# Loading the last three chunks of x by one transfer per partition quadrant, and issuing the first chunk from ScalarE

## The chip, the cores and the metric

One core of a Trainium2 chip. Times are microseconds of device time for one execution; lower is better. The profile's span (first to last instruction) is about 1.7 us shorter than the time.

## The reference, cut to what matters

```python
# x: (1, 384, 384, 384) bf16, dw: (1, 1, 384) bf16, pw: (384, 384) bf16
out = x * dw[0, 0]                          # k = 1: the depthwise part is a scaling of channels
return einsum('bhwc,cd->bhwd', out, pw)     # 147456 rows of 384 channels, times 384 x 384
```

113 MB come in and 113 MB go out. dw is folded into pw once, so the work is one large matrix product, read and written once.

## The kernel before

The 147456 rows are 288 supertiles of 512 rows. They are loaded and stored in chunks: groups of 1, 1, 2, 2, 4 supertiles at the start, tens in the middle, then 6, 4 and 3, 2, 1, 1, 1 at the end. Three x buffers and three output buffers, of ten supertiles each, are used in turn. VectorE transposes, TensorE multiplies, ScalarE evicts (copies the results from PSUM to the output buffer), and SyncE issues nearly all transfers, in program order on one queue. The code is cut and condensed.

```python
head, tail = [[1, 1, 2, 2, 4]], [[6, 4], [3, 2, 1, 1, 1]]
LMAX = 10; NR = 3; LONG = 3
...
def load_x(t):
    g, i, off, first, L = chunks[t]
    dst = Xs[g % NR][:, 4 * off : 4 * (off + L), :]
    rows = xf[512 * first : 512 * (first + L), :]
    if first + LONG < NS:
        src = rows.rearrange("(p s) c -> p (s c)", p=P)
        dst = dst.rearrange("p s c -> p (s c)")
    else:                                    # the last three chunks: rows of 768 B
        src = rows.rearrange("(a k q) c -> q a k c", k=4, q=4)
    if i == 0 and g >= NR:                   # until the buffer's old rows are transposed
        nc.sync.wait_ge(...)
    nc.sync.dma_start(dst, src).then_inc(s_x[g % NR][i], 16)

def store(t):
    ...
    nc.sync.wait_ge(s_a[je % 2], je // 2 + 2)          # the eviction of its last supertile
    nc.sync.dma_start(dst, src).then_inc(s_o[g % NR], 16)

nc.scalar.dma_start(dw_row[:], ...).then_inc(s_dw, 16)
nc.sync.dma_start(pw_n[:], ...).then_inc(s_pw, 16)
# then all loads and stores on nc.sync: a load when the group three before it is done,
# a store two supertiles after its chunk; at the end SyncE waits for all stores
for o in range(NR):
    nc.sync.wait_ge(s_o[o], 16 * sum(map(len, groups[o::NR])))
```

The last three chunks hold their rows in another order, so that their stores are contiguous (3072 B from each partition). Their loads pay for it with rows of 768 B.

## Time and profile before

| | before |
|---|---|
| time, median of the first three runs | 575.39 us |
| span of the profiled run | 573.7 us |
| TensorE's stream of 13824 matmuls | 7.18 to 569.0 us, idle 0.1 us |
| last eviction ends | 569.96 us |
| SyncE's wait for the stores at the very end | 2.0 us |

### The profile page before, as it was taken

The numbers are of one execution on the slowest core, as the hardware profiler recorded it, in microseconds if no ns is written. First come the engines' busy times: TensorE is split into PE (matmuls) and PEld (weight loads), VectorE is DVE, ScalarE is ACT, GpSimd is POOL, SyncE is SP. The second block draws the span as 40 slices with busy tenths as digits, with TensorE's granted clock in tenths as the row PEclk, the third lists the DMA queues.
The fourth block names the chain that finished last, engine by engine and source line by source line (L and its number), as shares of the span: only waits on it lengthen the run. The fifth ranks groups of instructions, "written<-read, shape, count | busy, mean of one in ns | idle before, by whom it ended". The sixth has DMA issues, their size and how long they took to land.

```text
span 573.7 us, 29706 instructions
## 1 busy us (share of the span) xinstructions
PE 567.3 (99%) x13869; PEld 414.9 (72%) x13869; DVE 509.3 (89%) x583; ACT 418.8 (73%) x296; POOL 0.9 (0%) x8
## 2 busy tenths in 40 slices
PE   8999999999999999999999999999999999999996
PEld 5777777777777777777777777777777777777774
DVE  6899999999999999999999999999999999999994
ACT  6777777777777777777777777777777777777775
POOL 0000000000000000000000000000000000000000
PEclk9999999999999999999999999999999999999999
DMA  8999999999999999999999999999999999994996
GB/s 324 432 409 417 430 397 430 444 424 422 399 408 416 384 397 436 398 383 395 432 398 384 395 429 390 393 401 429 402 385 419 401 390 397 425 394 149 402 408 251
DMA packets 25912, 226.88 MB, mean 395 GB/s; under 512 B 1197, under 2 KB 5678, under 8 KB 22062
## 3 DMA queue, kind: packets, MB, share of 16 engines
q1 hardware_dynamic: 25900, 226.79, 98.0%
q14 instruction: 9, 0.07, 0.0%
q8 instruction: 1, 0.02, 0.0%
q10 hardware_dynamic: 2, 0.00, 0.0%
HBM read 113.54 MB, written 113.25 MB: 395 GB/s over the span
## 4 chain that ended last, share of the span: by engine, by line
PE 98%; DMA 1%; ACT 0%; DVE 0%; issue 0%; SPq 0%
PE ps L166 97%; DMA pw_n<-in_pw_dram 1%; PE ps L216 1%; DMA out_dram<-O 0%; ACT O L307 0%; DVE O L304 0%; SPq L337 0%; SPq L100 0%
## 5 line engine op out<-in xcount | busy, mean ns | idle before, releaser
L166 PE MATMUL ps<-w_r,T 32*128 32x384 bf16 x13824 | 561.8, 321 | 0.1
L258 DVE STREAM_TRANSPOSE T<-X 128x384 uint32<-128x384 uint32 x576 | 506.2, 882 | 54.0 <-DMA X<-in_x_dram 2.4
L307 ACT CAST O<-ps 128x1536 bf16<-128x1536 f32 x288 | 413.5, 1436 | 147.9 <-PE ps L166 147.9
L166 PEld LDWEIGHTS ps<-w_r,T 32*128 32x128 bf16 x13824 | 412.9, 93 | 149.2 <-issue 0.7
L271 ACT CAST w_r<-ps 128x768 bf16<-128x768 f32 x5 | 3.7, 805 | 1.7 <-PE ps L216 1.6
L183 PE MATMUL ps<-zero 32*128 32x384 bf16 x24 | 2.6, 494 | 1.4 <-POOL zero L232 1.4
L304 DVE CAST O<-ps 128x768 bf16<-128x768 f32 x1 | 1.0, 958 | 3.0 <-DMA out_dram<-O 3.0
L216 PE MATMUL ps<-pw_n,sel_w 64*128 64x384 bf16 x18 | 3.0, 510 | 0.1
L183 PEld LDWEIGHTS ps<-zero 32*128 32x128 bf16 x24 | 0.7, 100 | 2.6 <-issue 2.6
L216 PEld LDWEIGHTS ps<-pw_n,sel_w 64*128 64x128 bf16 x18 | 1.2, 138 | 1.6 <-issue 1.2
L244 ACT ACT_TABLE_LOAD x1 | 1.3, 1283 | 1.5 <-SPq L100 1.5
L276 DVE TENSOR_REDUCE sel<-eye 128x64 f32<-128x128 bf16 x1 | 0.3, 290 | 1.8 <-POOL eye L234 1.8
L271 DVE CAST w_r<-ps 128x768 bf16<-128x768 f32 x1 | 1.0, 956 | 1.0 <-PE ps L216 1.0
L286 DVE TENSOR_SCALAR sel_w<-sel,dw_f 128x256 bf16<-128x256 f32 x3 | 0.9, 348 | 0.0
L283 DVE COPY dw_f<-ps 128x3 f32<-128x3 f32 x1 | 0.2, 161 | 0.8 <-PE ps L198 0.8
L198 PEld LDWEIGHTS ps<-ones,dw_row 1*128 1x128 bf16 x3 | 0.2, 98 | 0.2 <-issue 0.2
L244 ACT COPY warm<-warm 128x1 f32<-128x1 f32 x2 | 0.3, 188 | 0.0
L234 POOL TENSOR_SCALAR_AFFINE_SELECT eye<-ones 128x128 bf16<-128x128 bf16 x1 | 0.3, 292 | 0.1
L232 POOL MEMSET zero<- 128x192 uint32 x1 | 0.3, 258 | 0.0
L198 PE MATMUL ps<-ones,dw_row 1*128 1x1 bf16 x3 | 0.2, 159 | 0.0
L233 POOL MEMSET ones<- 128x128 bf16 x1 | 0.2, 204 | 0.0
L231 POOL MEMSET warm<- 128x3 f32 x1 | 0.1, 101 | 0.5 <-SPq L100 0.5
(4 smaller groups left out, 0.4 us busy)
## 6 DMA issues: line engine op xcount, KB each, us to landing
X<-in_x_dram SPq DMA_DIRECT2D x26, 3840.0 KB, 21.5
out_dram<-O SPq DMA_DIRECT2D x26, 3840.0 KB, 27.5
X<-in_x_dram SPq DMA_DIRECT2D x2, 1536.0 KB, 17.4
out_dram<-O SPq DMA_DIRECT2D x2, 1536.0 KB, 13.7
X<-in_x_dram SPq DMA_DIRECT2D x3, 768.0 KB, 8.8
out_dram<-O SPq DMA_DIRECT2D x3, 768.0 KB, 8.9
X<-in_x_dram SPq DMA_DIRECT2D x1, 2304.0 KB, 18.9
out_dram<-O SPq DMA_DIRECT2D x1, 2304.0 KB, 12.1
```

The source lines that it names most:

```text
L166: mm = nc.tensor.matmul(PS[s][:, q, :D], lhsT=Ts[s][32 * q : 32 * q + 32, b, par::2], rhs=w_r[32 * q : 32 * q + 32, b, par, :], start=(b, ...
L183: nc.tensor.matmul(PS[0][:, i, :D], lhsT=zero[32 * i : 32 * i + 32, 0:P], rhs=zero[32 * i : 32 * i + 32, :], start=True, stop=True, tile_p ...
L198: mm = nc.tensor.matmul(PS[1][:, 0, D + k : D + k + 1], lhsT=dw_row[:, P * k : P * k + P], rhs=ones[0:1, 0:1], start=True, stop=True,)
L216: mm = nc.tensor.matmul(PS[(k + 1) % 2][:, 2 * r + v, :D], lhsT=sel_w[64 * v : 64 * v + 64, k, r, :, :].rearrange("p q w -> p (q w)"), rhs ...
L232: nc.gpsimd.memset(zero[:].bitcast(U32), 0).then_inc(s_zero)
L234: nc.gpsimd.affine_select(out=eye[:], in_=ones[:], pattern=[[-1, P]], compare_op=mybir.AluOpType.is_equal, fill=0.0, base=0, channel_multi ...
L244: c = nc.scalar.copy(warm[:, s + 1 : s + 2], warm[:, 0:1])
L258: ins = nc.vector.transpose(out=Tw[:, 3 * h : 3 * h + 3], in_=Xw[:, :, j, 96 * h : 96 * h + 96].rearrange("p k (b w) -> p b k w", w=32),)
L271: o = nc.vector.tensor_copy(out, in_) if e == 0 else nc.scalar.copy(out, in_)
L286: nc.vector.tensor_scalar_mul(sel_w[:, k], sel[:].unsqueeze(2).to_broadcast([P, 2, 4, 32]), dw_f[:, k : k + 1]).then_inc(s_sw)
L304: e = nc.vector.tensor_copy(Ov[:, nq:4, j, :], PS[s][:, nq:4, :D])
L307: a = nc.scalar.copy(Ov[:, 0:nq, j, :], PS[s][:, 0:nq, :D])
```

## The change

The intent: the old loads of the last three chunks have q = 4 as slowest source dimension and run on four DMA engines, in a stretch in which the DMA moves 100 GB/s. With one transfer per quadrant (32 partitions) each runs on sixteen. The first chunk of x is issued by ScalarE, so that it need not wait behind pw's issue on SyncE.

```diff
-        def load_x(t):
+        def load_x(t, eng=nc.sync):
...
+            if first + LONG < NS:
+                src = rows.rearrange("(p s) c -> p (s c)", p=P)
+                eng.dma_start(dst.rearrange("p s c -> p (s c)"), src).then_inc(sem, 16)
+            else:
+                src = rows.rearrange("(a k q) c -> q a k c", k=4, q=4)
+                for q in range(4):
+                    nc.sync.dma_start(dst[32 * q : 32 * q + 32], src[q]).then_inc(sem, 16)
...
         nc.scalar.dma_start(dw_row[:], dw.rearrange("a e c -> a (e c)")).then_inc(s_dw, 16)
+        load_x(0, nc.scalar)
         nc.sync.dma_start(pw_n[:], pw.rearrange("(k p) d -> p k d", p=P)).then_inc(s_pw, 16)
...
-                    nc.vector.wait_ge(s_x[g % NR][i], 16 * sum(len(ls) > i for ls in groups[g % NR : g + 1 : NR]))
+                    nc.vector.wait_ge(s_x[g % NR][i], x_count[t])      # 64 per quadrant-loaded chunk
```

More of the change, by code (lines that the diff above doesn't have):

```diff
@@ L60 @@
     NT = len(chunks)
+    x_count = []
+    for t, (g, i, off, first, L) in enumerate(chunks):
+        n = 4 if first + LONG >= NS else 1
+        x_count.append(16 * n + max([x_count[u] for u in range(t) if chunks[u][0] % NR == g % NR and chunks[u][1] == i], default=0))
     g_end = [max(c[3] + c[4] for c in chunks if c[0] == g) - 1 for g in range(len(groups))]
@@ L104, in load_x @@
             rows = xf[512 * first : 512 * (first + L), :]
-            if first + LONG < NS:
-                src = rows.rearrange("(p s) c -> p (s c)", p=P)
-                dst = dst.rearrange("p s c -> p (s c)")
-            else:
-                src = rows.rearrange("(a k q) c -> q a k c", k=4, q=4)
+            sem = s_x[g % NR][i]
             if i == 0 and g >= NR:
@@ L112, in load_x @@
                 nc.sync.wait_ge(s_t[je % 2][1], je // 2 + 1)
-            nc.sync.dma_start(dst, src).then_inc(s_x[g % NR][i], 16)
+            if first + LONG < NS:
[5 more added lines that the diff above has]
+                    nc.sync.dma_start(dst[32 * q : 32 * q + 32], src[q]).then_inc(sem, 16)
         def store(t):
@@ L135 @@
         for t, (g, i, off, first, L) in enumerate(chunks):
-            todo.append((g_end[g - NR] if g >= NR else -1, load_x, t))
+            if t > 0:
+                todo.append((g_end[g - NR] if g >= NR else -1, load_x, t))
             todo.append((first + L + 1, store, t))
```

## The prediction

> **What bounds the kernel now.** I read the page first, then the chain of work that ended last, then the timeline of the first 16 us and the DMA view of the start and of the last 60 us, because the change touches only those two ends. From the page:
>
> ```profile
> span 573.7 us, 29706 instructions
> ...
> PE 567.3 (99%) x13869; PEld 414.9 (72%) x13869; DVE 509.3 (89%) x583; ACT 418.8 (73%) x296; POOL 0.9 (0%) x8
> ...
> L166 PE MATMUL ps<-w_r,T 32*128 32x384 bf16 x13824 | 561.8, 321 | 0.1
> L258 DVE STREAM_TRANSPOSE T<-X 128x384 uint32<-128x384 uint32 x576 | 506.2, 882 | 54.0 <-DMA X<-in_x_dram 2.4
> ```
>
> The matmul stream covers 561.8 of 573.7 us and its column of idle time holds 0.1 us. So nothing in the middle is waiting for x. The transposes idle 54.0 us, but only 2.4 of these for x, all near the start. The chain of waits in order of time gives the rest:
>
> ```profile
> 1.01 3.03 DMA pw_n<-in_pw_dram
> ...
> 4.09 2.96 PE ps L216 x18
> 7.05 0.12 issue
> 7.18 557.91 PE ps L166 x13728
> ...
> 566.57 2.46 DMA out_dram<-O
> 569.02 0.94 DVE O L304
> ```
>
> The end is: load of pw (1.01 to 4.04), 18 matmuls that build w_r (to 7.05), start of the stream at 7.18, 288 supertiles, last eviction, last store. A supertile is 557.91 us for 13728 matmuls of 48, thus 557.91 / 286 = 1.951 us. 7.18 + 288 x 1.951 = 569.0, which is where the last eviction starts (569.02, 0.94 long). The two-digit DMA step before it is an attribution to whichever semaphore came last; the eviction can only start when the matmuls are done, and it does so at just that time. After 569.96 come the last store's issue (570.06), its landing 2.3 us later and a close of about 1.3 us. The timed median is 575.39, 1.7 us over the span. So the time is: start of the stream + 561.8 + about 4.7 + 1.7. The change can act only on the start of the stream, on a stall inside it, or on the last store.
>
> The timeline of the start shows that the first chunk of x is not what starts the stream:
>
> ```profile
> 1.52 3.49 SPq L113 DMA_DIRECT2D X<-in_x_dram  x7
> ...
> 4.63 3.80 ACT L271 CAST w_r<-ps 128x768 bf16<-128x768 f32 x5 [1.56 <-PE ps L216]
> 4.96 0.96 DVE L271 CAST w_r<-ps 128x768 bf16<-128x768 f32 x1 [1.00 <-PE ps L216]
> 5.83 1.55 DVE L258 STREAM_TRANSPOSE T<-X 128x384 uint32<-128x384 uint32 x2
> ...
> 8.00 1.57 DVE L258 STREAM_TRANSPOSE T<-X 128x384 uint32<-128x384 uint32 x2 [0.62 <-DMA X<-in_x_dram]
> ```
>
> The first transposes follow VectorE's own cast of w_r without idle time; x's first chunk landed 3.5 us after its issue at 1.52, so at 5.0. The second chunk made VectorE wait 0.62 us, yet supertile 1 starts only at 9.13 and needs its first half of T by then; 8.00 + 0.88 (one transpose) = 8.9 is in time.
>
> The last three chunks: engine busy time by stretch, whose last two columns are the DMA share and GB/s:
>
> ```profile
> 516.00:520.00 4.00, 4.00 (x104) 2.95 (x100) 3.63 (x5) 2.88 (x2) 0.00 (x0) 1.00 0.78 309
> 520.00:524.00 4.00, 4.00 (x108) 2.94 (x100) 3.63 (x5) 2.88 (x2) 0.00 (x0) 1.00 0.31 89
> 524.00:528.00 4.00, 4.00 (x105) 2.93 (x101) 3.61 (x5) 2.88 (x2) 0.00 (x0) 1.00 0.34 99
> ```
>
> For some 12 us the DMA moves about 100 GB/s, with a share of 0.31 to 0.34, about five engines of 16, while TensorE is full. That is a large defect that costs nothing: the stream is at its full rate through it.
>
> **What the Trainium skill says.** "DMA: Bandwidth & Descriptors", section "Why a DMA increments its semaphore by 16 and not by 1", says that the number of DMA engines used is the largest one up to 16 that divides the slowest dimension of both access patterns. The old source has q = 4 slowest, so 4 engines; the new ones have 32 rows, so 16. The trace agrees: share 0.31, and 3 x 393 KB at about 100 GB/s is 11.8 us, as long as the dip. The same page, "Issuing engines are not separate DMA queues", says that transfers issued by different engines share the 16 DMA engines and that only issue time is saved. The trace of before has one load per queue at a time and can't show it. Its section "Queues, rings and completion order" says that each DMA engine takes turns between the queue rows it has work for; no run here shows it yet, and it is my main concern. "TensorE: Matmul & The Clock Gate", Part 1, says the array runs at half clock until a window of about 3.4 us was busy. The trace agrees in kind: the 18 building matmuls go in pairs 2.96 / 9 = 0.33 us apart, while four stream matmuls take 1.951 / 12 = 0.163 us, at equal width of 384 columns.
>
> **The change part by part.** First, the tail. Three issues become twelve. A load's issue takes about 0.45 us, so nine more are about 4 us on SyncE's queue. But one of the three old issues was held for 8.8 us and one for 4.4, and the five of that group took 14.91 us (511.42 to 526.33). I expect the new ones to be out by about 518, so the store behind them goes out some 8 us sooner than at 526.38. The loads should land about 10 us sooner. They are needed at about 559, two supertiles before their matmuls (7.18 + 285 x 1.951 = 563), and landed by about 532: 27 us of slack already. Stores do not gain at the end either: the last three small stores land 3.3, 2.6 and 2.3 us after issue, so the queue has no backlog by then. Worth to the time: 0, at most 0.1 us.
>
> Second, the start. What is removed is one issue (0.45 us) of SyncE, so that the chunks from the second on go out 0.5 us sooner; VectorE's 0.62 us wait shrinks, and TensorE does not notice: 0. What is added to ScalarE is one issue of 0.49 us (as for dw_row) ahead of its table load (1.49, 1.28 us) and two copies: ScalarE is ready at 3.6 and not at 3.1, and its first cast comes at 4.63: 0. The chunk itself is issued at 0.97 + 0.49 = 1.46 and not at 1.52: no gain.
>
> What moves is the order on the DMA engines. Before, x's first chunk stood behind pw on one queue. Now it stands on another. pw is the head of the critical chain, and of its packets only some have gone when the chunk comes:
>
> ```profile
> DMA packets 132, 0.10 MB, mean 169 GB/s; under 512 B 0, under 2 KB 132, under 8 KB 132
> ## 3 DMA queue, kind: packets, MB, share of 16 engines
> q1 hardware_dynamic: 132, 0.10, 75.3%
> ```
>
> This is 2.2 to 2.8 us. dw_row's packets came about 0.9 us after its issue began, so the chunk's should come at about 2.4 to 2.5. By then pw has moved 14 + some 66 of its 384 packets of 768 B; about 304 are left, 19 per engine. The chunk is 8 packets of 3072 B per engine, each about 0.124 us (81 packets at a share of 104.8% of 16 engines in 4.0 to 4.6 us). If the engines alternate, all eight go ahead of pw's last: 8 x 0.124 = 1.0 us later for pw, and so for the stream. If the engine prefers the older ring or the chunk starts later, less. I take 0.6 as the middle. Sum: tail 0, issue 0, sharing +0.6, so 575.39 + 0.6 = 576.0.
>
> **The rivals.** (a) Nothing: pw's descriptors are all queued before the chunk's, and the engines finish them first. For it: its issue ends at 1.46, when ScalarE's second begins. Then 575.3 to 575.5. (b) Full alternation: 576.4. (c) The clock: TensorE's filler ends at 4.02, just before pw lands at 4.04; a pause of up to 1 us there may cost the busy window, and the stream would start at half clock. The building matmuls ran slow until about 6.6 and the stream fast from its first, so the switch came late. Up to 3.4 us at half speed loses 1.7 us: 577 to 578 at worst. Against it: the pause is under a third of a window. (d) Gain: pw at the head of a less crowded queue, or a better place of the clock window: 575.0. (e) The tail as the bound: excluded by the full matmul stream in 520 to 528. A loss of 2% would be 11.5 us, more than the whole head before the stream; a gain of 2% would need the stream itself to speed up, which has no idle time to give.
>
> **Range and chances.** Weights of about a third each for nothing, part and full alternation, a fifth for some clock loss on top, a tenth for a small gain: 576.0, range 575.1 to 577.3. Within 2%: 0.985; faster 0.005; slower 0.01.
>
> **What would show it right or wrong.** Right: pw lands later than 3.03 us after issue by as much as the stream starts later than 7.18; packets on both queues between 2.4 and 4 us; still 1.951 us a supertile; the 520 to 528 dip gone, with no effect on the end. Wrong: pw at 3.0 us again (rival a); matmuls of the stream slow at first (c); a wait of TensorE on transposes in the stream; a last store that lands sooner or later by over 0.3 us.

## More of the kernel before

The queue's own waits of the kernel before (waiting engine and line, releaser: us in total, times, longest):

```profile
SPq L141 <- DMA out_dram<-O: 2.0, 1, 2.0
```

It is one wait, after the last issue, for all stores to land. It is the last piece of the span that the kernel's own work decides.

## The result, and the profile after

| | before | after |
|---|---|---|
| time, median (6 runs each) | 575.44 us | 577.26 us (577.11 to 577.34) |
| span of the profiled run | 573.7 us | 575.5 us |
| stream of matmuls starts | 7.18 us | 7.22 us |
| last eviction ends | 569.96 us | 570.01 us |
| SyncE's wait for the stores | 2.0 us | 3.7 us |

The ratio is 1.003, with a 95% interval of 1.0017 to 1.0043. A ratio is the mean time of the fast runs of one kernel over that of the other's of the same rounds, so not quite the ratio of the medians quoted. The change is 1.8 us slower: far inside 2%, but clear of the noise.

The chain of waits of the kernel after, in order of time (start, length, what):

```profile
1.03 3.06 DMA pw_n<-in_pw_dram
...
4.13 3.01 PE ps L225 x18
7.14 0.07 issue
7.22 557.91 PE ps L175 x13728
...
569.07 0.94 DVE O L313
```

Up to the last eviction it is the old chain, 0.04 us later: pw landed after 3.06 us, where it took 3.03. So almost all of the 1.8 us come after 570 us. The queue's own waits of the kernel after:

```profile
SPq L150 <- DMA out_dram<-O: 3.7, 1, 3.7
```

3.7 against 2.0 us in this last wait, plus 0.04 at the start, is the difference, but for rounding. The DMA view of 569 to 571 us shows whose landing it is (size, then us from issue to landing). Before:

```profile
out_dram<-O SPq DMA_DIRECT2D x1, 384.0 KB, 2.3
```

After:

```profile
out_dram<-O SPq DMA_DIRECT2D x1, 384.0 KB, 4.1
```

The same 384 KB, issued at 570.06 and 570.10 us, land 1.8 us later. Engine busy time by stretch of the kernel after (last columns: TensorE clock, DMA share, GB/s):

```profile
516.00:520.00 4.00, 4.00 (x107) 2.96 (x100) 3.63 (x5) 2.88 (x2) 0.00 (x0) 1.00 1.03 331
520.00:524.00 4.00, 4.00 (x108) 2.92 (x103) 3.63 (x5) 2.88 (x2) 0.00 (x0) 1.00 0.64 151
524.00:528.00 4.00, 4.00 (x104) 2.95 (x100) 3.63 (x5) 2.88 (x2) 0.00 (x0) 1.00 0.24 75
```

The dip that the change was to fill is still there. And SyncE's timeline shows that the twelve issues were not quick. Before:

```profile
511.42 14.91 SPq L113 DMA_DIRECT2D X<-in_x_dram  x5
526.38 4.41 SPq L128 DMA_DIRECT2D out_dram<-O  x1
```

After:

```profile
511.46 0.81 SPq L116 DMA_DIRECT2D X<-in_x_dram  x2
512.32 16.43 SPq L120 DMA_DIRECT2D X<-in_x_dram  x12
528.79 0.58 SPq L135 DMA_DIRECT2D out_dram<-O  x1
```

The twelve took 16.43 us, and the store behind them went out at 528.79, 2.4 us later than before.

Why should a store be slow at 570 when the loads were over at 535? The landing of a transfer is the last of its increments, and the trace has the time of each increment: sixteen for a transfer on sixteen DMA engines, one when each engine's share has landed. I sorted them. For the five transfers that matter, the first fifteen and the last stand like this (us; worked out from the increments in the two traces):

```text
                                  before                       after
transfer                     issued  15th   16th         issued  15th   16th
store, 3840 KB               476.9   496.1  505.4        476.9   497.0  505.0
load, three supertiles       511.4   519.1  528.7        511.5   520.9  528.4
store, 3840 KB               526.4   543.5  544.5        528.8   539.9  545.2
store, 3840 KB               535.4   552.6  553.6        535.4   549.3  555.7
last store, 384 KB           570.1   572.3  572.4        570.1   572.4  574.2
```

In both kernels one increment comes 6 to 10 us after the other fifteen, from the middle of the run on. In the kernel before this lag is all but gone after the four-engine loads. In the kernel after it is 5 to 6 us there and still 1.8 us at the last store (574.175 less 572.380). So the theory, L: **one DMA engine lags behind the other fifteen. The old loads used four engines, and this one was not among them; so it could catch up while they ran. The new ones give it a sixteenth of everything.** In the trace of the kernel after, each of the twelve quadrant loads has one late increment, the first of them at 530.9 and the last at 534.75 us. The transfer ahead of them was done on that engine at 530.7. So its share of the three chunks cost it 4.07 us.

The packed traces also hold the DMA packets, without the names of their engines, and they show the same. Between 522.5 and 526.4 us of the kernel before, 367 packets of 768 B (the four-engine loads) fill the time of 3.9 engines, and 12 packets of 9216 and 7680 B, of the transfers ahead of them, come one after the other, 0.32 to 0.36 us apart, and fill that of one more. In the kernel after, 12 packets of 3072 B come one at a time, 0.12 us apart, from 572.36 us on; 0.4 us after the end of the last one the last store has landed.

### The profile page after: what moved, and what is told of

Its sections match the earlier page's. It is cut to its first block, busy times and chain, and to the rows that moved or that the text cites. A ratio compares the mean times of both kernels' runs of the same rounds, so it can differ in the third digit from the quotient of the medians.

```text
span 575.5 us, 29715 instructions
## 1 busy us (share of the span) xinstructions
PE 567.4 (99%) x13869; PEld 415.0 (72%) x13869; DVE 510.9 (89%) x583; ACT 418.8 (73%) x296; POOL 0.9 (0%) x8
## 4 chain that ended last, share of the span: by engine, by line
PE 97%; DMA 1%; ACT 0%; DVE 0%; issue 0%; SPq 0%
PE ps L175 97%; DMA pw_n<-in_pw_dram 1%; PE ps L225 1%; DMA out_dram<-O 0%; ACT O L316 0%; DVE O L313 0%; SPq L346 0%; SPq L105 0%
```

## The experiments

The rivals were H (the second queue at the start costs the time), F (the form of a quadrant load costs, whichever engine), I (what costs is that the store behind the loads is issued late) and M (there is no single engine; it changes). Twelve kernels ran, in four calls; each call has its own runs of the kernel before, with medians of 575.53 to 575.61 us. All were correct.

| run | what | median us | ratio to before | last wait of SyncE, profiled run |
|---|---|---|---|---|
| e1 | ScalarE's issue alone | 575.86 | 0.9998 | 2.8 |
| e2 | quadrant loads alone | 577.39 | 1.0022 | 4.0 |
| e3 | quadrants, last chunk | 576.09 | 1.0002 | 2.4 |
| e4 | quadrants, last two | 576.48 | 1.0009 | 3.1 |
| f2 | e2, last stores on 15 engines | 578.32 | 1.0046 | 4.4 |
| f3 | e2, two quadrant loads doubled | 580.27 | 1.0073 | 6.9 |
| f4 | e2, a store ahead of the loads | 577.79 | 1.0031 | 5.1 |
| h1 | e2, pair load on 4 engines | 576.24 | 1.0008 | 3.0 |
| h2 | e2, pair load on 5 engines | 581.24 | 1.0095 | 8.0 |
| h3 | before, pair load on 4 engines | 580.18 | 1.0080 | 5.4 |

f1 and g1 are probes with one look each.

### e1_scalar_issue_only and e2_quadrants_only: which half of the change

e1 keeps the single transfers at the end; e2 takes the other half:

```diff
# e1
-        n = 4 if first + LONG >= NS else 1
+        n = 4 if first + QUAD >= NS else 1          # QUAD = 0: no chunk by quadrants
# e2
-        load_x(0, nc.scalar)
-            if t > 0:
-                todo.append((... load_x, t))
+            todo.append((... load_x, t))
```

> Only the first chunk's issue moves to ScalarE; the last three loads stay single transfers. Theory L (one DMA engine lags the other 15 by about 8 us in the steady state; the old four-engine loads left it out and let it catch up, the sixteen-engine loads don't): 575.4 to 575.5 us, start of the stream at 7.2, last store landing at 572.4. Rival H (the second queue costs the time, for example by sharing at the start or by a lasting disturbance of the rings): 577.2 us.

> Only the last three loads change; the first chunk is issued by SyncE as before. Theory L: 577.2 us (576.9 to 577.4), the last store's sixteenth landing 1.5 to 2 us after its fifteenth-but-one, last eviction still at 569.0. Rival H: 575.4 us.

e1 measured 575.86 us, ratio 0.9998, somewhat above L's 575.4 to 575.5; e2 577.39 us, ratio 1.0022 (1.0000 to 1.0043). H falls: the quadrant loads alone make the time of the whole change. The last wait in e2:

```profile
SPq L148 <- DMA out_dram<-O: 4.0, 1, 4.0
```

e1's four runs go from 575.52 to 576.64. Its profiled run (576.08 us) has a lag of 0.8 us at the last store, so the old form does not clear the lag fully in every run either. The runs of the kernel before scatter in the same way, 575.38 to 577.7.

### e3_quadrants_last_one and e4_quadrants_last_two: the dose

```diff
+                if first + QUAD >= NS:              # QUAD = 1, 2
+                    for q in range(4):
+                        nc.sync.dma_start(dst[32 * q : 32 * q + 32], src[q]).then_inc(sem, 16)
+                else:
+                    nc.sync.dma_start(dst, src).then_inc(sem, 16)
```

> Quadrant loads for the last chunk alone, the two before it as single four-engine transfers. Theory L: each chunk by quadrants costs the lagging engine 4.07/3 = 1.36 us (it needed 530.7 to 534.75 us for its share of three), so two fewer take 2.7 us off a lag of 1.8 at the end: none left, 575.4 to 575.6 us. Rival F (the form of the load, four issues and four waits of the last chunk, costs by itself): most of the 1.8 us, 576.5 to 577.2.

> Quadrant loads for the last two chunks. Theory L: 1.36 us less than for three: 575.7 to 576.1 us. Rival F: the same as with three, 577.2.

The medians are 576.09, 576.48 and (e2) 577.39 us for one, two and three chunks, beside 575.59 for none. The order is that of L, and F's step at the first chunk is absent. But one chunk cost 0.5 us, where L as I wrote it said 575.4 to 575.6 us and so 0.0 to 0.2, and two cost 0.9, where it said 575.7 to 576.1 us and so 0.3 to 0.7. The simple count of 1.36 us per chunk overstates what leaving one out gives back; the old form's own scatter (e1) may be a part of that. The intervals (for e3, 0.998 to 1.0025) are wider than these steps, so the order rests on the medians and on the last waits, 2.4 and 3.1 us.

### f1_width_probes and g1_width_probes_fine: which engine

Eight small loads of n rows to an unused tile, each with its own semaphore, ahead of the last three chunks. The reading of them takes it that a wider probe uses the engines of a narrower one and more:

```diff
+            if first + LONG == NS:
+                for w, n in enumerate(WIDTHS):
+                    some = rows.rearrange("(a k) c -> a k c", k=4)[:n, 0]
+                    nc.sync.dma_start(scratch[:n, w], some).then_inc(s_probe[w], 16)
```

> The kernel before with eight tiny extra loads (2, 4, 8, 10, 12, 14, 15 and 16 rows of 768 B to an unused tile) issued just before the last three chunks; only their landings matter, not the time. Theory L: one ring is still busy until about 530 us with the two loads ahead; [...]all probes that leave the lagging engine out land by about 523 us and all that include it at about 530 us or later. The step tells which engine it is, above the lowest four. Rival M (no single engine; the late increment is on changing engines): no such step, or late landings in the narrow probes too.

> The same probes with 3, 4, 5, 6, 7, 8, 9 and 16 rows. The first probes put the late landing between 4 rows (none) and 8 rows (one at 532.6 us), so the lagging engine is one of the fifth to eighth. Theory L: one step between two neighbouring widths, with exactly one landing after 530 us in every wider probe. If it lies between 7 and 8 rows, it is the eighth engine, number 7.

Increments of each probe, from the two traces; an early increment at the issue, which each probe but the one of 16 rows has, is left out:

```text
rows                           2   3   4   5   6   7   8   9  10  12  14  15  16
landings before 526 us         2   3   4   4   5   6   7   8   9  11  13  14  15
landings after 532 us          0   0   0   1   1   1   1   1   1   1   1   1   1
```

There is exactly one late landing in every probe of five rows and more, and none in those of four and fewer, in both runs (on 4, 8, 10 and 16 rows, which both have, they agree). A single step fits that order. So it is one engine, and in the order in which engines are used it is the fifth. M falls for these two runs, which were on two chips (15 and 7), so it is not a fault of one chip alone. The four-engine loads of the kernel before leave it out by one place.

f1's single time was 577.53 us with the last eviction 0.9 us later than before. It was not run for its time.

### f2_last_stores_fifteen: a wrong guess at the engine

Sent in the same call as f1, before I knew its answer; I had guessed the highest engine.

```diff
+                nc.sync.dma_start(dst[:120], src[:120]).then_inc(s_o[g % NR], 16)
+                nc.sync.dma_start(dst[120:], src[120:]).then_inc(s_o[g % NR], 16)
```

> Quadrant loads for three chunks as in the change, first chunk by SyncE; the last three stores are cut into 120 rows and 8 rows, so that the highest DMA engine has no part in them. Theory L with the highest engine as the lagging one: the lag has 3 x 0.98 us less to do, the end no longer waits for it: 575.7 to 576.0 us (one more issue of 0.35 us at the end). If the lagging engine is another one: 577.5 to 577.8 us.

578.32 us: not the highest engine. It is even 0.5 us above the range for that case. That fits what f1 showed: the fifth engine takes 8 of the 120 rows and one of the 8, so nine packets and not eight in each of the three stores. But no run isolates this.

### f3_quadrants_doubled: twice the suspected cost

```diff
+                for q in range(4 if first + 2 >= NS else 0):
+                    nc.sync.dma_start(dup[NS - 1 - first][32 * q : 32 * q + 32], src[q]).then_inc(s_dup, 16)
```

> Quadrant loads for three chunks, and the last two of them a second time to an unused tile. Theory L: two more chunk shares of 1.36 us on the lagging engine, which is never idle from there to the end: 577.2 + 2.7 = 579.9 us, about 2.2 us of tolerance for its idle time. Rival I (what costs is that the store behind the loads is issued late, 528.8 instead of 526.4): eight more issues of 0.6 us, nothing proportional, and the other fifteen engines late too.

580.27 us against 579.9 expected. The last wait grew to 6.9 us. At the last store of the profiled run fifteen engines had landed by 574.1 us and the lagging one by 577.7, so in the main it is the one engine, though the others were over 1 us late as well.

### f4_store_before_loads: the late issue

```diff
+            late = 2.5 if first + LONG >= NS else 0
+            todo.append((g_end[g - NR] + late if g >= NR else -1, load_x, t))
```

> The quadrant loads come behind the 3.84 MB store instead of ahead of it, so that this store is issued near 516 us and not at 528.8. Theory L: the lagging engine has the same bytes and no idle time to lose, so 577.0 to 577.5 us. Rival I (late issue of the store): 575.4 to 575.7 us.

577.79 us (577.04 to 578.58), with that store issued at 515.87 us. Expected by L: 577.0 to 577.5, so 0.3 below it, by I: 575.4 to 575.7. The twelve loads now took 25.15 us to issue and the next store went out at 541.5 and not at 535.4, so this run alone does not refute I; still, a store issued 13 us earlier gave nothing back. What speaks against I is the increments. In the kernel after the lagging engine ended its last quadrant share at 534.75 us, 6 us after the store behind it was issued (528.79), and in f4 at 546.78, 5 us after (541.5). An earlier issue would have found it busy.

### h1_pair_load_four and h2_pair_load_five: spare the fifth engine, or load it

The quadrant loads stay as in the change. The load of two supertiles ahead of them (6144 B per partition) is cut so that it uses four engines or five: 124 = 4 x 31, 125 = 5 x 25.

```diff
-                eng.dma_start(dst.rearrange("p s c -> p (s c)"), src).then_inc(sem, 16)
+                for lo, hi in ((0, 124), (124, P)) if first + LONG + 2 == NS else ((0, P),):    # h2: 125
+                    eng.dma_start(dst[lo:hi], src[lo:hi]).then_inc(sem, 16)
```

> Quadrant loads for three chunks, first chunk by SyncE; the load of the two-chunk piece just ahead of them is cut into 124 and 4 partitions, so that it uses the four lowest DMA engines alone. The fine probes put the lagging engine at the fifth place (a late landing from five rows up). Theory L: that engine is spared 8 packets of 6144 B at about 0.235 us, 1.9 us, which is all of its lag at the end: 575.4 to 575.9 us, with the quadrant loads as in the change. Rival F (the quadrant form costs by itself): 577.4 us.

> The same with a cut of 125 and 3 partitions: five engines, the lagging one among them. Theory L: it gets 25 packets and not 8, 17 x 0.235 = 4.0 us more: about 581.4 us (580 to 582.5). If the lagging engine isn't the fifth, or the number of engines in itself is what counts: as with four engines, 575.4 to 576.

One partition more makes the difference between 576.24 and 581.24 us. h2 met its number (581.4). h1 fell short: it gave back 1.15 us of e2's 577.39 and not all of it; in its profiled run a lag of 1.0 us was left at the last store. This pair also answers F: with the quadrant form unchanged, the time follows what the fifth engine is given. The last waits in h1 and in h2:

```profile
SPq L151 <- DMA out_dram<-O: 3.0, 1, 3.0
SPq L151 <- DMA out_dram<-O: 8.0, 1, 8.0
```

In h2 the last five stores leave one late increment each, at 573.70, 575.58, 576.50, 577.43 and 578.36 us; the other fifteen engines were done with the last store at 572.8, the four low ones, which had been given at least as much of the pair load as the fifth, among them. The last four are 0.92 to 0.93 us apart (575.58 to 578.36): the engine works its way through what stands in its queue, 8 packets of 3072 B for each of the last three stores, with no pause.

### h3_before_pair_four: more of the same relief

The kernel before, with the same cut at 124, tried as a version that might beat both.

> The kernel before with the two-chunk piece cut into 124 and 4 partitions. Theory L: the lag of the fifth engine is already gone at the end of the kernel before, so there is nothing to gain: 575.3 to 575.6 us. Perhaps fewer of the runs at 576 and above. If the four low engines get too far behind, up to 577.

580.18 us: wrong, beyond even my "up to 577". In the profiled run the last two increments of the stores stand at 575.05 and 575.57, and the late ones are spread from 573.1 us on: now several engines are late. The reading that the four low engines, with a quarter of four chunks each, have become the slow ones fits the spread, but the increments do not name their engines. So no run was clearly faster than the kernel before. That it sits in a narrow place, in which the four engines take just about what the fifth needs to be spared, is my reading of the two failures on either side.

## Why the prediction was right or wrong

The time fell into the range (577.26 in 575.1 to 577.3), barely, and the class was right. The sum was not: both of its steps failed. (Nor do its weights add up: three thirds, and a tenth besides.) That the range held it, by 0.04 us, is luck: its upper end was set for losses at the start and at the clock, and the loss came at the end. The prediction's own sign of being wrong, "a last store that lands sooner or later by over 0.3 us", came true.

- **What bounds the kernel** held: 1.951 us a supertile, no wait of TensorE, and every run's last eviction at about 569 to 570 us (568.8 to 569.9 at its start).
- **The start, "sharing +0.6"** failed. pw landed after 3.06 and not 3.03 us and the stream began 0.04 us later: rival (a), "nothing", in size. The time at which the chunk's packets come, estimated at 2.4 to 2.5 us, was a wrong term. The DMA view of the kernel after, 2.6 to 3.2 us (packets, MB, share of 16 engines):

```profile
q1 hardware_dynamic: 223, 0.17, 92.5%
```

and 3.2 to 4.1 us:

```profile
q10 hardware_dynamic: 94, 0.29, 79.5%
q1 hardware_dynamic: 119, 0.10, 30.9%
```

ScalarE's queue (q10) moved nothing of the chunk until 3.2 us, though its issue began at 1.53. By then 313 of pw's 384 packets had gone. The other 71 shared the time with the chunk's, and the last of pw's began at 3.66 us, as it had before. Whether any engine took turns between the queues the packets do not tell, as they don't name their engines. I took dw_row's 0.9 us from issue to first packet as the delay of any transfer; for this one it was 1.7 us (first packet at 3.25). A packet of 3072 B was read as 0.124 us from 81 packets, of which 15 were of under 512 B; the records of these packets say 0.12 to 0.15.
- **The clock (rival c)** failed: no pause, and the stream ran at full rate from its first matmuls.
- **The tail, "0, at most 0.1 us"** failed, and this is the step that mattered: from its issue the last store took 4.07 us to land and not 2.31, +1.76 us. "The queue has no backlog by then" was read from landings of the kernel before, where it is true; I carried it over to the kernel after. The DMA share is a mean over 16 engines, and it hid that one of them had been 6 to 10 us behind since the middle of the run. A sign of it stood in the prediction: a share of "about five engines of 16", where the loads had four. The fifth was the lagging one, still at the transfers ahead of them. Rival (e), the tail, was excluded from the matmul stream in 520 to 528, which says nothing about what is still queued at 570. The old four-engine loads were called "a large defect that costs nothing". They were the pause in which that engine recovered.
- **The loads "about 10 us sooner", the issues "out by about 518", the dip gone**: all three failed. The last load landed at 534.75 and not 535.36 us, the issues lasted until 528.7, and the share in 520 to 528 was 0.64 and 0.24. The prediction's "landed by about 532" was misread (535.36, so 24 us of slack and not 27). The loads still had 24 us to spare until about 559. That SyncE is held because the one engine's queue is full is likely, as issues ran at 0.6 to 2.8 us each while most engines idled (share 0.24 in 524 to 528); no run tests it.
- **The gain of 0.5 us for the later first chunks** held and, as said, was worth nothing: VectorE's waits for x fell from 2.4 us to none listed, and TensorE did not notice.

Where the lag comes from, the record shows in part. Between 90 and 150 us of the kernel before it grew with each large store (0.9, 2.2, 3.5, 4.8 us) and not with the loads between them (0.9, 2.2, 3.5). The packets of these stores (7680 B) fall into two kinds: between 85 and 500 us 94% of them take 0.291 us, and 635 of 10948, close to a sixteenth, take 0.33 us on average. These start 0.30 us apart or more all through, as those of one engine would, 28 to 32 to a store (each engine's share is 32). 32 x 0.04 = 1.3 us, and the lag grew by 1.3 us at each of these stores.

Open: why these packets are slower (no run tells the engine from the rows and partitions that it serves), and what holds the distance at about 8 us. The lag is there in every trace looked at, in both forms of the kernel.

## What to carry to other kernels

A mean DMA share says nothing about the slowest of the sixteen engines, and a transfer is as late as the slowest: compare the last increment of each transfer with the fifteen before it, above all for the last store. Before spreading a badly spread transfer, ask which engine it leaves alone and whether that one needs the rest; 25 packets of 6144 B (154 KB) given to it or spared it were worth 5 us at the end here (h1 and h2). And a stretch that looks wasteful while the engine that sets the time is full may be what another part of the kernel recovers in.

## What the Trainium skill lacked or had wrong

- "DMA: Bandwidth & Descriptors", section "Rules for kernel authors", advises to use all 16 engines by putting a dimension that is a multiple of 16 outermost. Here the transfers on sixteen engines made the kernel 1.8 us slower (577.26 against 575.44), since one engine had no time to spare; the page has no word on leaving one out on purpose.
- The same page, section "Latency and other measured facts", names DMA engines 7 and 15 as usually slower than the others, with a guessed cause that it limits to transfers issued from GpSimd; here all were issued by SyncE and ScalarE. So it is not refuted, but it lacks this case: the late one was the fifth in order of use (one late landing from five rows up, none to four), in two runs on two chips, which is engine 4 if, as the page's section "Why a DMA increments its semaphore by 16 and not by 1" says, the lowest-numbered ones are used.
- Nothing was wrong with the rule for the number of engines in that last section; it agrees with all probes: n rows gave n landings and one early increment, 16 rows gave 16; the load cut at 124 partitions and the one cut at 125 gave 10 increments each, as 4 + 1 and 4 + 1, and 5 + 1 and 3 + 1, would.
- No page says how far one engine can fall behind in a long run or what stops it: it reached 9.6 us here (load of three supertiles, kernel before), and issues of 32-partition loads on SyncE then took up to 2.8 us each instead of about 0.45.
